# Gated rows transposed in 32x32 squares on VectorE, with transfers between partitions, and two steps of the z stage in another order

## The chip, the cores and the metric

The kernel runs on one core of one Trainium2 chip. A core has five engines that run their own instruction queues and wait for one another through semaphores: TensorE (PE; its weight loads are shown apart as PEld), VectorE (DVE), ScalarE (ACT), GpSimd (POOL) and SyncE (SP), which here issues nearly all transfers between DRAM and the on-chip memory SBUF. Products of TensorE land in PSUM, eight banks per partition. The metric is device time in microseconds; lower is better.

## The reference

A block of a transformer, all in float32: attention with 32 heads on a normalised x, added to x, then a gated MLP (gMLP) on the normalised sum. The change lies in the second half:

```python
h = x + _A_ref(_layernorm(x, axis=-1), A_wqkv, A_wo)
h2 = h + _B_ref(_layernorm(h, axis=-1), B_w_in, B_w_sp, B_b_sp, B_w_out)

def _B_ref(x, w_in, w_sp, b_sp, w_out):      # S = 2048 rows, D = 512, Fh = 688
    z = _gelu(jnp.einsum("bsd,df->bsf", x, w_in))
    z1 = z[..., :Fh]
    z2 = _layernorm(z[..., Fh:], axis=-1)
    g = jnp.einsum("ts,bsf->btf", w_sp, z2) + b_sp[None, :, None]
    return jnp.einsum("bsf,fd->bsd", z1 * g, w_out)
```

## The kernel before

Three stages follow one another. The first, attention, is not touched. Rows of x are handled in 16 blocks of 128 (`NB`); block p and block p+8 form pair p. Numbers in float32 are multiplied as sums of two float16 parts, a high and a low one, with three products each (`mm3`, lines 106 to 109; its lines 107, 108 and 109 are the three matmuls).

**The second stage** (loop over k at line 1242) takes the row blocks in the order 0, 1, 8, 9, 2, 10, 3, 11 and so on to 7, 15. For step k it makes h for the block two steps ahead (`make_h`), makes z for its own block in four pieces of 344 columns (`make_z(sb, 1, 0)`, `(1, 1)`, `(0, 0)`, `(0, 1)`: the first index is 1 for the half that is normalised, 0 for the half z1), and transposes the next block's normalised h on TensorE (`turn`, line 1175), which ScalarE and VectorE split into the parts hT (lines 98 and 104). Normalising needs 1/sqrt of a variance, a chain of some ten small VectorE instructions (`rstd_of`, lines 114 to 126, then nb at line 766) before ScalarE applies it; for h that gives hn (line 1268). `gate_z` (line 1203) does the same for z: z1 is stored to DRAM (z_scr, issued by ScalarE), the chain runs on VectorE, ScalarE normalises z2 (line 1212), and GpSimd mostly forms sums, differences and float16 parts of it, tiles b11, t1, t2, b22, t3, b21, n4, which are the operands of the spatial product in Strassen-like form (two levels of 2x2 blocks, seven products). One of those subtractions, for b21 of the lower block of a pair, is kept in the list `subs` and run on VectorE in the next step.

**The last stage** (loop over p) runs over the eight pairs. For a pair TensorE makes seven products of 24 matmuls (`product`), named after their operands: b11, t1, t2, b22, t3, b21, n4, into three PSUM banks A, C, B, the later ones adding to what stands there. Each consumes one 512 KB operand from a ring (`op`, nine buffers), and at its end asks for the operand eight products ahead. ScalarE and VectorE empty the banks, GpSimd multiplies with z1; the two gated rows of the pair stand in `pr` (row index w = 0, 1). Columns 0 to 383 are half 0, the rest half 1. For each half: `level` finds the largest magnitude per row (a reduction and three small instructions on VectorE), `raise_` scales the rows by a power of two on ScalarE, `turn` transposes three 128x128 blocks per row on TensorE into PSUM (line 1379; for half 1 GpSimd first copies 64 columns, so that the last block is whole), `split` makes the float16 parts pT from PSUM (high part on ScalarE, line 1387, low part on VectorE, lines 1388 and 1391), `multiply` multiplies them with w_out into a PSUM bank (acc, two buffers), and `gather` adds the result to h on VectorE (line 1408), which `store` writes out.

The order of the instructions on each engine, in both stages, is the order in which the code is written (`manual_schedule`); no scheduler moves them. A pair's `turn(1)` stands at its own end, behind n4, and its `multiply(1)`, `turn(0)` and `multiply(0)` stand in the next pair, behind products b11 and t1. Every transfer waits, besides its data, for the transfer issued eight places before it, since eight semaphores are used in turn.

Of the kernel before, what the change touches and what calls it, by code (L numbers as in the profile page):

```python
# [8 lines left out]
F32 = mybir.dt.float32  # L9
F32R = mybir.dt.float32r  # L10
BF = mybir.dt.bfloat16
F16 = mybir.dt.float16
# [47 lines left out]
def block_kernel(ctx: ExitStack, tc: tile.TileContext, x, wqkv, wo, w_in, w_sp4, b_sp, w_out, out):  # L60
# [1103 lines left out]
    with ExitStack() as mid:  # L1164
# [33 lines left out]
            else:  # L1198
                sub(nc.gpsimd if el == "pool" else nc.vector)

        subs = []

        def gate_z(sb, meanwhile):

# [33 lines left out]
        with tc.manual_schedule(engines={E.PE, E.Activation, E.DVE, E.Pool, E.SP}):  # L1238
# [3 lines left out]
            for k in range(NB):  # L1242
                sb, new = row[k], row.get(k + 2)
                if new is not None:
                    for _ in make_h(new, ps.tile([P, 512], F32, name="acc")):
                        pass
                if k + 3 < NB:
                    split_o(row[k + 3])
                new_z(sb)
                make_z(sb, 1, 0)  # L1250
                if k + 1 < NB and k != NB - 2:
                    turn(row[k + 1])
                if subs:
                    subs.pop()(nc.vector)
                if new is not None:
                    mv, rs = scale_h(new)
                    nb = minus_mean(e2, mv, rs)
                make_z(sb, 1, 1)
                if k == NB - 2:
                    turn(row[k + 1])  # L1260
                for c in range(2):
                    nc.vector.bn_stats(zst[sb][:, c, :], zs[sb][1][:, c * FC:(c + 1) * FC])
                make_z(sb, 0, 0)
                make_z(sb, 0, 1)
                hTs.pop(sb)
                if new is not None:
                    hns[new] = e2.tile([P, D], F32, name="hn", bufs=3)
                    nc.scalar.activation(hns[new], xrs.pop(new), AF.Identity, bias=nb, scale=rs)
                if k == 1:
                    invert()  # L1270
                if k >= NB - 8:
                    ask()

                def meanwhile():
                    if k + 4 < NB:
                        asked.pop(0)()
                    if k + 5 < NB:
                        asked.append(load_o(row[k + 5]))

                gate_z(sb, meanwhile)  # L1280
    early.close()
    late.close()

# [1 line left out]
    with ExitStack() as fin:  # L1285
# [52 lines left out]
        class Rows:  # L1338
# [26 lines left out]
            def lower(self, half, *which):  # L1365

                for w in which:
                    d = self.downs[half, w]
                    nc.vector.tensor_scalar(d, d, 2.0 ** -14, w_down, op0=ALU.mult, op1=ALU.mult)

            def turn(self, half, w):

                if half:
# [7 lines left out]
            def split(self, half, w):  # L1381

                tp, n = self.turned.pop((half, w)), 3 - half
                if half not in self.pT:
                    self.pT[half] = [f2.tile([P, 2, 3, P], F16, name=f"pT{half}{i}") for i in range(2)]
                hi, lo = self.pT[half]
                nc.scalar.activation(hi[:, w], tp[:, :3], AF.Copy)
                nc.vector.tensor_sub(lo[:, w, :n], tp[:, :n], hi[:, w, :n])
# [36 lines left out]
        with tc.manual_schedule(engines={E.PE, E.Activation, E.DVE, E.Pool, E.SP}):  # L1425
# [9 lines left out]
            for p in range(HB):  # L1435
# [8 lines left out]

                product(A, "b11")
                nc.scalar.activation(p1, A, AF.Identity, bias=bt)
                if p:
                    accs = [before.multiply(1, w) for w in range(2)]
                    for w in range(2):
                        before.turn(0, w)  # L1450
                        before.gather(1, w, accs[w])
                        before.split(0, w)
                    before.lower(0, 0, 1)
                product(C, "t1")
                nc.scalar.activation(q5, C, AF.Identity, bias=bb)
                if p:
                    accs = [before.multiply(0, w) for w in range(2)]
                    for w in range(2):
                        before.gather(0, w, accs[w])
                        before.store(w)  # L1460
                else:
                    weigh_w()
                product(A, "t2", False)
                nc.scalar.activation(v, A, AF.Identity, bias=bt)
                product(C, "b22", False)
                nc.vector.tensor_add(right, C, v)  # L1466
                nc.gpsimd.tensor_mul(right, right, z1t[:, FC:])  # L1467
                if not p:
                    measure_w()
                product(A, "t3", False)  # L1470
                nc.vector.tensor_add(br, A, q5)
                (nc.vector if last else nc.gpsimd).tensor_mul(br, br, z1b[:, FC:])
                now.level(1, 0, 1)
                now.raise_(1, 0, 1)
                product(B, "b21")
                nc.vector.tensor_add(left, B, p1)
                (nc.vector if last else nc.gpsimd).tensor_mul(left, left, z1t[:, :FC])
                if last:
                    now.level(0, 0)
                    for w in range(2):  # L1480
# [1 line left out]
                        now.split(1, w)  # L1482
                    now.lower(1, 0, 1)
                    now.raise_(0, 0)
                product(A, "n4", False)
                nc.vector.scalar_tensor_tensor(bl, A, bb, z1b[:, :FC], op0=ALU.add, op1=ALU.mult)
                if last:
                    now.level(0, 1)
                    now.raise_(0, 1)
                else:  # L1490
                    now.level(0, 0, 1)
                    for w in range(2):
                        now.turn(1, w)
                        now.split(1, w)
                    now.lower(1, 0, 1)
                    now.raise_(0, 0, 1)
            accs = [now.multiply(1, 0)]
            now.turn(0, 0)
            now.split(0, 0)
# [42 lines left out]
```

## Time and profile before

| what | us |
|---|---|
| median of 3 runs (lowest, highest) | 1726.86 (1726.46, 1728.48) |
| the profiled execution | 1726.86 |
| its span, first to last instruction | 1725.1 |
| busy: TensorE / VectorE / ScalarE / GpSimd | 1708.8 / 1438.4 / 1318.7 / 815.5 |
| attention, up to the first block of h turned (about) | 0 to 1295 |
| second stage: first turn (1294.60) to the start of b11 (1455.22) | 161 |
| last stage: to the end of the span | 270 |
| one pair of the last stage (turn to turn, 1513.28 to 1546.4) | 33.15 |
| granted TensorE clock | 1.000 |

A row of a timeline has the start, the duration, the engine, the line of the kernel, the operation, the tiles written and read, the shape and a count of like instructions drawn together; in brackets stands how long the engine was idle before it, and on whom it waited. A row that groups instructions has, behind the bar, busy us in total, the mean in ns and the idle time in front of them; where three numbers stand with slashes, they are the least, the median and the largest duration in ns, then the first and last start. A row of waits has the engine and tile that waited, the one waited for, the sum in us, the number of times and the longest. SPq and ACTq are the queues in which transfers are issued; a duration there is that of the issue.

### The profile page before, as it was taken

Reading aid. Unit: us, or ns where it says so; the run is one execution under the profiler, and the core shown is the slowest. Engines: PE = TensorE matmul, PEld = TensorE weight load, DVE = VectorE, ACT = ScalarE, POOL = GpSimd, SP = SyncE. Lnnn points to the kernel's source line nnn. Section 1 sums busy time; section 2 is a strip of 40 time slices with the busy share of each in tenths; the row PEclk is TensorE's granted clock in tenths of the full one; section 3 lists DMA queues with packets and bytes.
Section 4 is the critical chain, followed back from the end, with each engine's and each line's share of the span. In section 5 each row is a group of like instructions: output and inputs, shape, how many; then the busy total and the mean of one; then the engine's idle time right before and its main releaser. Section 6 shows DMA issues by size and latency. Waiting matters only on the chain.

```text
span 1725.1 us, 36747 instructions
## 1 busy us (share of the span) xinstructions
PE 1708.8 (99%) x13583; PEld 653.4 (38%) x13583; DVE 1438.4 (83%) x3030; ACT 1318.7 (76%) x2598; POOL 815.5 (47%) x1076
## 2 busy tenths in 40 slices
PE   9999999999999999999999999999999999999999
PEld 4433222222222222222222222222216566666665
DVE  7688999999999999999999999999927886433234
ACT  4334999999999999999999999999994554221111
POOL 1231867776672267687677866400013766110010
PEclk9999999999999999999999999999999999999999
DMA  5534332342231234344345343300124464654540
GB/s 183 162 97 144 101 88 69 100 98 81 75 71 27 60 105 117 113 149 135 103 121 146 115 147 103 80 20 12 45 51 135 136 184 159 228 179 145 170 139 25
DMA packets 183932, 190.51 MB, mean 110 GB/s; under 512 B 65704, under 2 KB 134632, under 8 KB 183752
## 3 DMA queue, kind: packets, MB, share of 16 engines
q1 hardware_dynamic: 181448, 182.53, 36.2%
q10 hardware_dynamic: 2304, 5.64, 0.8%
q8 instruction: 106, 1.74, 0.4%
q14 instruction: 74, 0.61, 0.1%
HBM read 122.10 MB, written 65.93 MB: 109 GB/s over the span
## 4 chain that ended last, share of the span: by engine, by line
PE 76%; DVE 15%; DMA 3%; ACT 2%; issue 2%; POOL 2%; SPq 1%; DVEq 0%; ACTq 0%; POOLq 0%
PE pv L828 26%; PE s L803 17%; PE m L223 9%; DVE mx L228 7%; PE acc L107 4%; PE g L109 4%; PE g L108 4%; PE g L107 4%; PE acc L109 3%; PE acc L108 3%; DVE ab L237 1%; DMA rc<-r_scr 1%; DVE og L838 1%; DVE rs_t L124 1%; DVE rs_u L126 1%
## 5 line engine op out<-in xcount | busy, mean ns | idle before, releaser
L812 ACT ACTIVATE pt<-s 128x512 f32<-128x512 f32 x1968 | 1006.3, 637 | 5.1 <-PE m L223 4.0
L228 DVE TENSOR_REDUCE mx<-m 128x1 f32<-128x512 f32 x1510 | 947.5, 682 | 12.6 <-PE m L223 3.9
L803 PE MATMUL s<-qst,kst 50*128 50x512 f16 x2048 | 604.3, 379 | 0.2
L828 PE MATMUL pv<-pt,vst 128*32 128x256 f32 (+1 forms) x6056 | 598.1, 466 | 4.1 <-DVE og L838 1.3
L223 PE MATMUL m<-kst,qst 48*128 48x512 f16 x1510 | 452.4, 381 | 0.0
L803 PEld LDWEIGHTS <-kst 50*128 50x128 f16 x2048 | 131.9, 94 | 352.1 <-issue 323.7
L828 PEld LDWEIGHTS pv<-pt,vst 128*32 128x32 f32 x6056 | 119.5, 108 | 290.3 <-issue 276.9
L223 PEld LDWEIGHTS <-qst 48*128 48x128 f16 x2048 | 159.2, 93 | 173.7 <-issue 124.3
L223 PE MATMUL m<-uvs,qst 48*128 48x512 f16 x504 | 190.5, 380 | 0.3 <-DVE mx L228 0.3
L245 POOL TENSOR_SCALAR nm<-nm 128x16 f32<-128x16 f32 x32 | 6.6, 206 | 359.7 <-DVE nm L242 359.7
L237 DVE CUSTOM_DVE_ANT_0 ab<-m,ab 128x512 f32<-128x512 f32 x252 | 170.5, 677 | 2.7 <-ACT ab L233 2.7
L233 ACT ACTIVATE ab<-m 128x512 f32<-128x512 f32 x252 | 157.3, 624 | 16.5 <-PE m L223 15.8
L989 POOL TENSOR_TENSOR op<-raw,op 128x512 f16<-128x512 f32 x80 | 92.9, 1161 | 6.0
L1467 POOL TENSOR_TENSOR pr<-pr,z 128x344 f32<-128x344 f32 x8 | 7.3, 912 | 176.9 <-DVE pr L1466 173.0
L912 POOL TENSOR_TENSOR raw<-raw 128x512 f32<-128x512 f32 (+1 forms) x84 | 83.3, 991 | 6.7
L917 POOL TENSOR_TENSOR acc_sp<-acc_sp,raw 128x512 f32<-128x512 f32 x63 | 80.5, 1277 | 4.5
L107 PE MATMUL acc<-wi,hT 128*128 128x344 f16 x256 | 79.1, 309 | 1.4 <-ACT hT L98 1.4
L1362 ACT ACTIVATE pr<-pr,up 128x304 f32<-128x304 f32 (+1 forms) x32 | 17.0, 574 | 81.9 <-DVE up L1316 81.9
L109 PE MATMUL acc<-wi,hT 128*128 128x344 f16 x256 | 79.1, 309 | 0.3 <-DVE hT L104 0.3
L108 PE MATMUL acc<-wi,hT 128*128 128x344 f16 x256 | 79.1, 309 | 0.0
L1408 DVE SCALAR_TENSOR_TENSOR h<-acc,low,h 128x512 f32<-128x512 f32 (+1 forms) x33 | 24.1, 732 | 45.8 <-PE acc L109 32.5
L909 POOL TENSOR_SCALAR raw<-raw 128x512 f32<-128x512 f32 (+1 forms) x88 | 52.3, 594 | 19.5 <-DMA raw<-in_wqkv 12.2
(240 smaller groups left out, 2280.1 us busy)
## 6 DMA issues: line engine op xcount, KB each, us to landing
raw<-in_w_sp SPq DMA_DIRECT2D x128, 256.0 KB
s_scr<-op SPq DMA_DIRECT2D x64, 256.0 KB
op<-s_scr SPq DMA_DIRECT2D x32, 512.0 KB
a_scr<-op SPq DMA_DIRECT2D x48, 256.0 KB
op<-a_scr SPq DMA_DIRECT2D x24, 512.0 KB
o_scr<-og SPq DMA_DIRECT2D x64, 128.0 KB
qst<-q_scr SPq DMA_DIRECT2D x192, 32.0 KB
kst<-k_scr SPq DMA_DIRECT2D x48, 128.0 KB
```

What stands on the lines that cost most here:

```text
L107: nc.tensor.matmul(ps, lh, rh, start=first, stop=False, **kw)
L108: nc.tensor.matmul(ps, lh, rl, start=False, stop=False, **kw)
L109: nc.tensor.matmul(ps, ll, rh, start=False, stop=last, **kw)
L223: nc.tensor.matmul(acc, q[r, p, c], keys[r, p], start=True, stop=True)
L228: nc.vector.reduce_max(at(t, e if t else e - 1), acc, axis=AX.X)
L233: nc.scalar.activation(ab[0], acc, AF.Abs)
L237: nc.vector.tensor_tensor_reduce(ab[0], acc, ab[0], 0.5, LOW, ALU.add, ALU.max, at(0, 0))
L803: nc.tensor.matmul(s, kst[hg % 2][r, p, kb * P:(kb + 1) * P], qst[hg * NQ + qb][r, p, :], start=True, stop=True)
L812: nc.scalar.activation(pts[p, kb][:, t, :], s, AF.Exp, scale=scales_[hg // 2])
L828: nc.tensor.matmul(pv[0][32 * j:32 * j + 32, a:b], vst[hg % 2][:, c:c + 32], pts[j % 2, kb][:, j // 2, a:b], start=kb == 0, stop=kb == NB - 1,
L912: pool.tensor_mul(got[0] if n else acc, got[0], got[0])
L989: chores.append((lambda: pool.tensor_sub(t[0][:, 1], of(), t[0][:, 0]), TT))
```

## The change

In the last stage, pairs 0 to 6 no longer transpose on TensorE. `squares` transposes the 32x32 squares of the scaled rows on VectorE, within groups of 32 partitions, into one tile for the pair; `send` issues 16 transfers of 48 KB from SBUF to SBUF that bring each square to the partitions where it belongs (`whole`); `hi` and `lo` make the float16 parts from there, on ScalarE and VectorE. The rows are still multiplied with w_out during the next pair, but behind product b21 rather than behind b11 and t1, and stored behind n4. Pair 7 still transposes on TensorE. The tiles pT have one buffer each instead of two.

In the second stage the late subtraction of b21 (`subs`) runs behind the 1/sqrt chain of h rather than ahead of it, and the gate work of the third last block (k = 13, block 14) runs in step k = 14, behind the turn of the last block, instead of at the end of its own step.

```diff
@@ -1198,7 +1198,7 @@
             else:
                 sub(nc.gpsimd if el == "pool" else nc.vector)
 
-        subs = []
+        subs, put_off = [], []
 
         def gate_z(sb, meanwhile):
 
@@ -1250,14 +1250,15 @@
                 make_z(sb, 1, 0)
                 if k + 1 < NB and k != NB - 2:
                     turn(row[k + 1])
-                if subs:
-                    subs.pop()(nc.vector)
                 if new is not None:
                     mv, rs = scale_h(new)
                     nb = minus_mean(e2, mv, rs)
+                if subs:
+                    subs.pop()(nc.vector)
                 make_z(sb, 1, 1)
                 if k == NB - 2:
                     turn(row[k + 1])
+                    put_off.pop()()
                 for c in range(2):
                     nc.vector.bn_stats(zst[sb][:, c, :], zs[sb][1][:, c * FC:(c + 1) * FC])
                 make_z(sb, 0, 0)
@@ -1271,13 +1272,16 @@
                 if k >= NB - 8:
                     ask()
 
-                def meanwhile():
+                def meanwhile(k=k):
                     if k + 4 < NB:
                         asked.pop(0)()
                     if k + 5 < NB:
                         asked.append(load_o(row[k + 5]))
 
-                gate_z(sb, meanwhile)
+                if k == NB - 3:
+                    put_off.append(lambda sb=sb, then=meanwhile: gate_z(sb, then))
+                else:
+                    gate_z(sb, meanwhile)
     early.close()
     late.close()
 
@@ -1368,6 +1372,49 @@
                     d = self.downs[half, w]
                     nc.vector.tensor_scalar(d, d, 2.0 ** -14, w_down, op0=ALU.mult, op1=ALU.mult)
 
+            def squares(self, half):
+
+                if half:
+                    self.sq = f2.tile([P, 4, 2, 2, 3, 32], F32, name="squares", bufs=1)
+                t = self.sq[:, :, half]
+                if half:
+                    for w in range(2):
+                        nc.vector.transpose(t[:, :, w, :2].rearrange("p q i a -> p i q a"),
+                                            self.pr[:, w, HF:HF + 2 * P])
+                    for q in (0, 2):
+                        nc.vector.transpose(t[:, q:q + 2, :, 2].rearrange("p q w a -> p w q a"),
+                                            self.pr[:, :, FH - TW:FH])
+                else:
+                    nc.vector.transpose(t.rearrange("p q w i a -> p (w i) q a"), self.pr[:, :, :HF])
+
+            def send(self):
+
+                self.whole = f2.tile([P, 4, 2, 2, 3, 32], F32, name="whole", bufs=1)
+                for j in range(4):
+                    for q in range(4):
+                        nc.sync.dma_start(self.whole[32 * q:32 * q + 32, j], self.sq[32 * j:32 * j + 32, q])
+
+            def hi(self, half):
+
+                src = self.whole[:, :, half].rearrange("p j w i a -> p (w i) j a")
+                self.pT[half] = [f2.tile([P, 2, 3, P], F16, name=f"pT{half}{i}", bufs=1) for i in range(2)]
+                nc.scalar.activation(self.pT[half][0].rearrange("p w i (j a) -> p (w i) j a", a=32), src, AF.Copy)
+
+            def lo(self, half):
+
+                src, (hi, lo) = self.whole[:, :, half], [
+                    t.rearrange("p w i (j a) -> p w i j a", a=32) for t in self.pT[half]]
+                if not half:
+                    lo, src, hi = [t.rearrange(f"p {d} -> p (w i) j a")
+                                   for t, d in ((lo, "w i j a"), (src, "j w i a"), (hi, "w i j a"))]
+                    nc.vector.tensor_sub(lo, src, hi)
+                    return
+                src = src.rearrange("p j w i a -> p w i j a")
+                for w in range(2):
+                    nc.vector.tensor_sub(lo[:, w, :2], src[:, w, :2], hi[:, w, :2])
+                t = hi[TW:, :, 2]
+                nc.vector.tensor_sub(t, src[TW:, :, 2], t)
+
             def turn(self, half, w):
 
                 if half:
@@ -1382,7 +1429,7 @@
 
                 tp, n = self.turned.pop((half, w)), 3 - half
                 if half not in self.pT:
-                    self.pT[half] = [f2.tile([P, 2, 3, P], F16, name=f"pT{half}{i}") for i in range(2)]
+                    self.pT[half] = [f2.tile([P, 2, 3, P], F16, name=f"pT{half}{i}", bufs=1) for i in range(2)]
                 hi, lo = self.pT[half]
                 nc.scalar.activation(hi[:, w], tp[:, :3], AF.Copy)
                 nc.vector.tensor_sub(lo[:, w, :n], tp[:, :n], hi[:, w, :n])
@@ -1444,37 +1491,40 @@
 
                 product(A, "b11")
                 nc.scalar.activation(p1, A, AF.Identity, bias=bt)
-                if p:
-                    accs = [before.multiply(1, w) for w in range(2)]
-                    for w in range(2):
-                        before.turn(0, w)
-                        before.gather(1, w, accs[w])
-                        before.split(0, w)
-                    before.lower(0, 0, 1)
                 product(C, "t1")
                 nc.scalar.activation(q5, C, AF.Identity, bias=bb)
-                if p:
-                    accs = [before.multiply(0, w) for w in range(2)]
-                    for w in range(2):
-                        before.gather(0, w, accs[w])
-                        before.store(w)
-                else:
+                if not p:
                     weigh_w()
                 product(A, "t2", False)
                 nc.scalar.activation(v, A, AF.Identity, bias=bt)
+                if p:
+                    before.lower(1, 0, 1)
+                    before.lower(0, 0, 1)
                 product(C, "b22", False)
                 nc.vector.tensor_add(right, C, v)
                 nc.gpsimd.tensor_mul(right, right, z1t[:, FC:])
-                if not p:
+                if p:
+                    before.hi(1)
+                    before.hi(0)
+                else:
                     measure_w()
                 product(A, "t3", False)
                 nc.vector.tensor_add(br, A, q5)
                 (nc.vector if last else nc.gpsimd).tensor_mul(br, br, z1b[:, FC:])
+                if p:
+                    before.lo(1)
+                    before.lo(0)
                 now.level(1, 0, 1)
                 now.raise_(1, 0, 1)
+                if not last:
+                    now.squares(1)
                 product(B, "b21")
                 nc.vector.tensor_add(left, B, p1)
                 (nc.vector if last else nc.gpsimd).tensor_mul(left, left, z1t[:, :FC])
+                if p:
+                    accs = [before.multiply(1, w) for w in range(2)]
+                    for w in range(2):
+                        before.gather(1, w, accs[w])
                 if last:
                     now.level(0, 0)
                     for w in range(2):
@@ -1482,18 +1532,23 @@
                         now.split(1, w)
                     now.lower(1, 0, 1)
                     now.raise_(0, 0)
+                if p:
+                    accs = [before.multiply(0, w) for w in range(2)]
+                    for w in range(2):
+                        before.gather(0, w, accs[w])
                 product(A, "n4", False)
                 nc.vector.scalar_tensor_tensor(bl, A, bb, z1b[:, :FC], op0=ALU.add, op1=ALU.mult)
+                if p:
+                    for w in range(2):
+                        before.store(w)
                 if last:
                     now.level(0, 1)
                     now.raise_(0, 1)
                 else:
                     now.level(0, 0, 1)
-                    for w in range(2):
-                        now.turn(1, w)
-                        now.split(1, w)
-                    now.lower(1, 0, 1)
                     now.raise_(0, 0, 1)
+                    now.squares(0)
+                    now.send()
             accs = [now.multiply(1, 0)]
             now.turn(0, 0)
             now.split(0, 0)
```

Three places show how the instructions now stand.

VectorE in one pair of the last stage, before, from the eviction br of product t3 (pr<-g,q) over the level of half 1, the eviction left (pr<-g,p) and the eviction bl, to the level of half 0:

```order
L1471 TENSOR_TENSOR pr<-g,q_23672 128x344
L1351 TENSOR_REDUCE low_23870<-pr 128x2
L1313 TENSOR_SCALAR low_23870<-low_23870 128x2
L1314 TENSOR_SCALAR low_23870<-low_23870 128x2
L1316 TENSOR_SCALAR up_23871<-low_23870 128x2
L1476 TENSOR_TENSOR pr<-g,p_23670 128x344
L1486 SCALAR_TENSOR_TENSOR pr<-g,fig_1843,z_23357 128x344
L1351 TENSOR_REDUCE low_23933<-pr 128x2
```

Now, from the same eviction br to the first gather (h<-acc):

```order
L1512 TENSOR_TENSOR pr<-g,q_23676 128x344
L1414 TENSOR_TENSOR pT_23791<-whole,pT_23790 128x256 x2
L1416 TENSOR_TENSOR pT_23790<-whole,pT_23790 64x2x128
L1410 TENSOR_TENSOR pT_23794<-whole,pT_23793 128x768
L1355 TENSOR_REDUCE low_23828<-pr 128x2
L1317 TENSOR_SCALAR low_23828<-low_23828 128x2
L1318 TENSOR_SCALAR low_23828<-low_23828 128x2
L1320 TENSOR_SCALAR up_23829<-low_23828 128x2
L1382 STREAM_TRANSPOSE squares<-pr 128x2x4x32 x2
L1385 STREAM_TRANSPOSE squares<-pr 128x2x2x32 x2
L1522 TENSOR_TENSOR pr<-g,p_23674 128x344
L1455 SCALAR_TENSOR_TENSOR h_23090<-acc,low_23524,h_23090 128x512
```

Behind br now stand the four low parts of the pair before, read from whole, and behind the level the four transposes; left and the first gather come after them.

SP's queue over one pair, before (z and h are loads for the next pair, op the operands, out_y the stores):

```order
L1421 DMA z_23355<-z_scr 128x688
L1421 DMA z_23357<-z_scr 128x688
L1421 DMA h_23359<-h_scr 128x512
L1421 DMA h_23361<-h_scr 128x512
L1161 DMA op<-s_2_scr 128x2048 x2
L1411 DMA out_y<-h_23082 128x512
L1411 DMA out_y<-h_23084 128x512
L1161 DMA op<-s_2_scr 128x2048 x2
L1161 DMA op<-a_2_scr 128x2048 x2
L1161 DMA op<-a_3_scr 128x2048
```

Now:

```order
L1395 DMA whole<-squares 32x384 x16
L1468 DMA z_23358<-z_scr 128x688
L1468 DMA z_23360<-z_scr 128x688
L1468 DMA h_23362<-h_scr 128x512
L1468 DMA h_23364<-h_scr 128x512
L1161 DMA op<-s_2_scr 128x2048 x4
L1161 DMA op<-a_2_scr 128x2048 x2
L1161 DMA op<-a_3_scr 128x2048
L1458 DMA out_y<-h_23082 128x512
L1458 DMA out_y<-h_23084 128x512
```

The 16 transfers of the pair before stand ahead of the loads, and the stores have moved behind the pair's last operand.

ScalarE in step k = 14 of the second stage, before (hn of the last block; then the gate of step 13: store, normalising, two casts; then z and hT of the last block):

```order
L1268 ACTIVATE hn<-xr,nb,rs_u 128x512
L1207 DMA z_scr<-z_22714 128x688
L1212 ACTIVATE z_22715<-z_22715,nb,rs_u 128x688
L1194 CAST b_0_20668<-z_22715 128x344
L1194 CAST b_0_20666<-z_22715 128x344
L1190 ACTIVATE z_22840<-acc,fig_1841 128x344 x2
L98 ACTIVATE hT_22876<-tp 128x512
```

Now:

```order
L1269 ACTIVATE hn<-xr,nb,rs_u 128x512
L1190 ACTIVATE z_22807<-acc,fig_1841 128x344 x2
L98 ACTIVATE hT_22842<-tp 128x512
L1207 DMA z_scr<-z_22714 128x688
L1212 ACTIVATE z_22715<-z_22715,nb,rs_u 128x688
L1194 CAST b_0_20668<-z_22715 128x344
L1194 CAST b_0_20666<-z_22715 128x344
```

The gate's four instructions have moved behind hT of the last block.

## The prediction

> **What bounds the kernel now.** Read first, the waits of TensorE over the second stage and the stretches of the last one (columns: PE, its weight loads, VectorE, ScalarE, GpSimd busy us, then granted clock, DMA share, GB/s):
>
> ```profile
> span 1725.1 us, 36747 instructions
> PE tp L1175 <- ACT hn L1268: 1.6, 5, 0.7
> PE acc L107 <- ACT hT L98: 1.4, 1, 1.4
> PE acc L109 <- DVE hT L104: 0.3, 1, 0.3
> ...
> 1500.00:1550.00 50.00, 50.00 (x334) 32.69 (x332) 16.66 (x41) 8.41 (x18) 6.18 (x10) 1.00 0.52 169
> 1650.00:1700.00 50.00, 50.00 (x317) 31.11 (x315) 15.01 (x35) 8.01 (x16) 3.09 (x5) 1.00 0.25 88
> ```
>
> The last stage is TensorE from end to end: it never waits there, at clock 1.00, while VectorE is busy a third of the time. So an instruction taken off TensorE is worth its full length, and a wait given to TensorE costs its full length. In the second stage TensorE does wait, a little. The timeline of TensorE at one pair's end gives the prices:
>
> ```profile
> 1509.78 0.31 PE L107 MATMUL g<-n,op 128*128 128x344 f16 x1
> ...
> 1513.28 0.82 PE L1379 MATMUL tp<-ident,pr 128*128 128x128 f32 x6
> 1513.93 0.31 PE L107 MATMUL g<-b,op 128*128 128x344 f16 x1
> ...
> 1517.43 0.38 PE L107 MATMUL acc<-wu,pT 128*128 128x512 f16 x1
> ...
> 1520.88 0.82 PE L1379 MATMUL tp<-ident,pr 128*128 128x128 f32 x6
> ```
>
> By starts, since ends are modelled: a product of 24 matmuls takes 1513.28-1509.78 = 3.50 us, six transposes 0.65, the 16 matmuls of multiply(1) for both rows 3.45 (0.216 each). The 18 of multiply(0) then take 3.89.
>
> **Removed: the transposes.** Pairs 0 to 6 lose 12 each, fourteen groups of six: 14 x 0.65 = 9.1 us off TensorE. The GpSimd copies that go with them ran beside it and are worth nothing.
>
> **Added: a line of work on VectorE, between t3 and the second multiply.** After product t3 VectorE now runs br, four subtractions (lo), level(1), the transposes in squares(1), left, and only then gather(1,0). With two banks for acc, multiply(0,0) cannot start before gather(1,0) has emptied the first. So I time that line, with T the start of b11, from this piece of the timelines:
>
> ```profile
> 1506.28 0.31 PE L107 MATMUL g<-b,op 128*128 128x344 f16 x1
> 1506.48 0.52 DVE L1471 TENSOR_TENSOR pr<-g,q 128x344 f32<-128x344 f32 x1 [2.91 <-PE g L109]
> 1507.07 0.91 POOL L1472 TENSOR_TENSOR pr<-pr,z 128x344 f32<-128x344 f32 x1 [2.51 <-DVE pr L1471]
> 1508.02 0.79 DVE L1351 TENSOR_REDUCE low<-pr 128x2 f32<-128x608 f32 x1 [1.02 <-POOL pr L1472]
> 1509.25 0.17 DVE L1316 TENSOR_SCALAR up<-low 128x2 int32<-128x2 int32 x1
> 1509.51 0.99 ACT L1362 ACTIVATE pr<-pr,up 128x304 f32<-128x304 f32 x2 [9.49 <-DVE up L1316]
> ...
> L1388 DVE TENSOR_TENSOR pT<-tp,pT 128x256 f16<-128x256 f32 x16 | 6.7, 421 | 0.2
> L1351 DVE TENSOR_REDUCE low<-pr 128x2 f32<-128x768 f32 x7 | 6.7, 953 | 0.7
> L1351 DVE TENSOR_REDUCE low<-pr 128x2 f32<-128x608 f32 x8 | 6.3, 786 | 7.5 <-POOL pr L1472 7.4
> L1408 DVE SCALAR_TENSOR_TENSOR h<-acc,low,h 128x512 f32<-128x512 f32 x31 | 23.2, 748 | 44.6 <-PE acc L109 31.3 <-PE acc L1403 13.1
> L1195 DVE TENSOR_TENSOR b<-z,b x7: 516/1094/1096, 1335.7 to 1446.4; 128x344 f16<-128x344 f32 x7
> ```
>
> t3 ends at T+17.5 (five products); br starts 0.2 later (1506.48 against 1506.28) and ends at T+18.2. The four lo, three of 256 elements per partition at 0.42 and one of 768 at 0.95, make 2.2: T+20.4. But lo now reads two tiles in SBUF, where before one was in PSUM, and GpSimd's product for br (0.91, from 0.59 after br's start) falls on it. The last row is the nearest: the same kind of subtraction took 516 ns alone and 1094 in its median case, with GpSimd at work. I add one GpSimd product, 0.85: T+21.25. The reduction and its three small instructions take 1.40 (1508.02 to 1509.42): T+22.65; ScalarE's two scalings start 0.1 later and end at T+23.75. squares(1) has four transposes of 256, 256, 128 and 128 elements per partition; the first hides behind the second scaling.
>
> Their price is not in the trace for this type. Lower bound: the two reductions differ by 160 elements and 0.167 us, so 0.00104 per element on a base of 0.15, giving 0.42 and 0.28. Upper bound: twice the part that grows, 0.69 and 0.42. The nearest row is a transpose of half the width, which stands by the base and shows no fill time, so I take the lower:
>
> ```profile
> L259 DVE STREAM_TRANSPOSE mturned<-mparts x32: 199/201/211, 143.9 to 1252.2; 128x32 f16<-128x32 f16 x32
> ```
>
> The Trainium skill (Vector Engine (DVE) Microarchitecture Reference, section 3.8) says that the transposing front end sustains one element per cycle per lane; by that the sum is mine, and no run here shows it for four bytes yet.
>
> Three more transposes, 0.98, bring T+24.7; left 0.5: T+25.2; gather(1,0) 0.75: T+25.95. TensorE ended b21 at T+21.0 and multiply(1) at T+24.45. It waits till about T+25.9 (instructions overlap by up to 0.1): **1.4 us per pair**. After that gathers fit between multiplies (1.94 each), and left, bl and the pair's other evictions have slack. Without the collision the wait is 0.55; with the dear transposes 2.2.
>
> This holds for pairs 1 to 6. Pair 0 has nothing to multiply. In pair 7 there is no squares(1) and GpSimd is idle beside lo: br and its product end at T+18.8, lo at T+21.0, level(1) at T+22.3, left and its product T+23.3, gather(1,0) T+24.1, before T+24.45. So 6 x 1.4 = 8.4 us are given back.
>
> The Trainium skill (SBUF — State Buffer, Who interferes with whom) speaks against this change: a VectorE instruction with two SBUF inputs and a GpSimd instruction that reads SBUF exclude each other, and the later one waits for the whole of the other. The 1094 ns agree. By the rule the wait is 1.4 a pair, without it 0.55, and the sum 5 us lower.
>
> **Added: 16 transfers per pair, and what they pass.** squares(0) waits for n4's end, bl, level(0) and the scaling:
>
> ```profile
> 1513.48 0.57 DVE L1486 SCALAR_TENSOR_TENSOR pr<-g,fig,z 128x344 f32<-128x344 f32 x1 [2.98 <-PE g L109]
> 1515.82 1.12 ACT L1362 ACTIVATE pr<-pr,up 128x384 f32<-128x384 f32 x2 [1.14 <-DVE up L1316]
> ...
> 1514.45 0.90 SPq L1421 DMA_DIRECT2D h<-h_scr  x2
> ...
> 1252.40 0.33 SPq L260 DMA_DIRECT2D m_scr<-mturned  x1
> 1254.66 1.34 SPq L263 DMA_DIRECT2D qst<-m_scr  x2
> ```
>
> Scaling ends 3.7 after n4 (1516.94-1513.28); the 768-element transpose adds 0.95 (as the reduction): T+4.7 of the next pair. Sixteen issues at 0.33 to 0.45 make 6.4, and a small transfer that another waits for is there 2.3 after its issue (1252.40 to 1254.66): all landed near T+13.3. Each also waits for the transfer eight places ahead; at 2.3 us that one is done. hi(1) and hi(0) follow on ScalarE, about 1.05 each, done at T+15.4, well ahead of T+18.2. Behind the 16 in SP's queue stand the z and h loads and four operand loads, now some 10 us later; operands are asked eight products (28 us) ahead and z, h are for the next pair, so that costs nothing; were operands late, it would show as TensorE waiting on op.
>
> **Moved: the second stage.** The late subtraction of b21 stood ahead of the 1/sqrt chain; now it stands behind it:
>
> ```profile
> 1428.65 1.09 DVE L1195 TENSOR_TENSOR b<-z,b 128x344 f16<-128x344 f32 x1
> 1431.92 0.21 DVE L766 TENSOR_SCALAR nb<-rs_u,mv 128x1 f32<-128x1 f32 x1
> 1432.17 0.81 ACT L1268 ACTIVATE hn<-xr,nb,rs_u 128x512 f32<-128x512 f32 x1 [2.85 <-DVE nb L766]
> ...
> 1432.50 0.31 PE L109 MATMUL acc<-wi,hT 128*128 128x344 f16 x1
> 1433.03 0.44 PE L1175 MATMUL tp<-ident,hn 128*128 128x128 f32 x2 [0.23 <-ACT hn L1268]
> ```
>
> hn comes 1.0 us earlier, more than the longest of the five waits (0.7). A shown wait is short by 0.16, since matmuls start every 0.146 but are drawn 0.31 long: 1.6 + 5 x 0.16 = 2.4 us. The subtraction itself has a pair's time to spare.
>
> The gate of row 13 is put behind the turn of row 15. ScalarE did it ahead of hT(15):
>
> ```profile
> 1441.12 0.33 ACTq L1207 DMA_DIRECT2D z_scr<-z  x1
> 1444.50 0.96 ACT L1212 ACTIVATE z<-z,nb,rs_u 128x688 f32<-128x688 f32 x1 [2.58 <-DVE nb L766]
> 1447.13 0.59 ACT L98 ACTIVATE hT<-tp 128x512 f16<-128x512 f32 x1
> 1447.78 0.32 PE L107 MATMUL acc<-wi,hT 128*128 128x344 f16 x1 [1.40 <-ACT hT L98]
> 1453.54 0.84 POOL L1195 TENSOR_TENSOR b<-z,b 128x344 f16<-128x344 f32 x1
> ```
>
> hT(15) can start once its transposes are done, near 1442.9, so both hT waits go: 1.40 + 0.26 + 2 x 0.16 = 2.0. What is late next: the gate's 1/sqrt starts after hT's lo, 2.3 us later, and with it GpSimd's parts. The gate's store of z moves too, from 1441.12 to about 1443.6; the one z tile that it reads is rewritten near 1448.5, so it stays covered. Row 13's b21 subtraction moves to the next row's turn, long before the last stage's b21. b11's last low part, 1453.54 to 1454.38 here, then comes near 1456.6, while TensorE, 2 us ahead, wants it near 1456.4: 0.2 is given back. Gain 4.2; bounds 0 (if GpSimd is later than that) and 4.4.
>
> **Sum.** 1725.1 - 9.1 + 8.4 - 4.2 = 1720.2 us of span. The profiled execution took 1726.86, 1.8 over its span and equal to the median: **1722.0 us**. About 0.2% (3.5 us) is what a measurement can tell from no change, so this is just faster.
>
> **Rivals.** *VectorE's line is cheaper* (18%): no collision, so 0.55 per pair: 1722.0 - 5.1 = 1717; hidden wholly, 1713.6. For it: GpSimd could be held back instead. Against: level(1) needs that very product.
>
> *Dear squares* (20%): transposes at twice the part per element, or VectorE keeping GpSimd out through all four lo, so that level(1) starts 1 us later: 2.2 to 2.4 a pair, 1727 to 1728. For it: nothing in the trace prices either.
>
> *The transfers land late* (14%, the slower side). It decides from T+17: each us beyond delays hi, lo and all behind it by 1 us, six times. If each took 7 us, as the 1280 KB load of raw_w does, the second eight wait for the first: T+4.7+7+2.8+7 = T+21.5, lo starts at T+22.6, 4.4 late less the 0.85 collision: 6 x 3.6 = 21 more, 1743. Against: DMA share is half.
>
> ```profile
> 1455.52 0.38 SPq L1430 DMA_DIRECT2D raw_w<-in_w_out  x1
> 1463.57 3.65 DVE L1322 TENSOR_REDUCE w<-raw_w 128x1 f32<-128x512 f32 x6 [3.29 <-DMA raw_w<-in_w_out]
> ```
>
> *The moved gate gains nothing* (6%): GpSimd's parts hold b11 as long as the waits were: 1726.
>
> **Chances.** My case has 42%, and its own range 1719 to 1725 from a wait of 1.0 to 1.9; six parts in seven of it lie under 1723.4. Faster: 36 + 18 = 54%. Within 0.2%: 6 + 20 + 6 = 32%. Slower: 14%. The range from 1715 to 1730 holds all but late transfers and a wholly hidden line.
>
> **What would show it.** L1379's count falls from 96 to 12. TensorE's waits in the last stage: one of about 1.4 us per pair on gather (h), six times, ahead of multiply(0,0); none on op, pT or p. The lo subtractions of 256 elements: one of the three near 1.3 us, or GpSimd's product near 1.3 or longer. Transposes of 256 elements 0.42 us against 0.69. In the second stage the waits on hn and hT are gone. Wrong if TensorE waits for hi (late transfers), or if gather(1,0) ends before multiply(1) does.

## The result, and the profile after

The changed kernel takes **1720.37 us** (median of 6 runs, 1719.88 to 1720.95) where the kernel before took 1727.07 beside it (6 runs, 1725.97 to 1728.48): ratio 0.9963, 95% interval 0.9953 to 0.9973. The forecast was 1722.0 us, with 1719 to 1725 as its own case's range; the gain is 6.7 us where 4.9 was forecast.

The waits of TensorE in the changed kernel, whose span is now 1718.6 us, first over the second stage (1285 to 1452 us), then, behind the dots, over the last one (from 1452 us); columns: what waited for what, us in total, times, longest:

```profile
PE acc L109 <- DVE hT L104: 0.3, 1, 0.3
PE acc L745 <- DVE og L838: 0.2, 1, 0.2
...
PE acc L107 <- DVE h L1455: 5.0, 6, 1.0
```

The five waits on hn and the wait of 1.4 us on hT(15) are gone. A wait on hT of 0.3 is still there, but it is another: it stands ahead of z of row 14, at 1437.90 us. In the last stage there are six waits, all on h (the gather), none on pT, op or p. Each is 0.16 longer than shown, since matmuls start every 0.216 us and are drawn 0.38: 5.0 + 6 x 0.16 = 6.0 us, 1.0 a pair.

Two stretches of the last stage of the changed kernel (PE, its weight loads, VectorE, ScalarE, GpSimd busy us, clock, DMA share, GB/s):

```profile
1500.00:1550.00 50.00, 48.23 (x302) 29.38 (x301) 20.91 (x48) 7.68 (x15) 3.76 (x4) 1.00 0.54 199
1650.00:1700.00 50.00, 49.23 (x314) 30.63 (x312) 20.62 (x46) 9.31 (x16) 4.36 (x6) 1.00 0.38 126
```

TensorE, busy throughout before, now has holes: 1.8 us in the first stretch, which holds two of the waits, and 0.8 in the second, which holds one. The groups of the instructions that the change touches (busy us, mean ns | idle before, and who ended it), over the last stage:

```profile
L1426 PE MATMUL tp<-ident,pr 128*128 128x128 f32 x12 | 1.8, 272 | 0.0
L1382 DVE STREAM_TRANSPOSE squares<-pr 128x256 f32<-128x256 f32 x14 | 6.2, 446 | 4.8 <-ACT pr L1366 4.8
L1385 DVE STREAM_TRANSPOSE squares<-pr 128x128 f32<-128x128 f32 x14 | 3.2, 270 | 0.0
L1388 DVE STREAM_TRANSPOSE squares<-pr 128x768 f32<-128x768 f32 x7 | 6.8, 978 | 8.7 <-ACT pr L1366 8.7
L1414 DVE TENSOR_TENSOR pT<-whole,pT 128x256 f16<-128x256 f32 x14 | 9.2, 702 | 0.6 <-ACT pT L1401 0.5
L1513 POOL TENSOR_TENSOR pr<-pr,z 128x344 f32<-128x344 f32 x7 | 7.1, 1021 | 14.9 <-DVE pr L1512 14.8
```

Of 96 transposes on TensorE 12 are left, those of pair 7. VectorE's transposes cost the lower bound of the prediction. The lo subtractions of 256 elements take 702 ns in the mean where 421 was the price of the like subtraction before, and GpSimd's product 1021 where it took 912: the two run into each other, as the experiment on lo below shows.

One pair's line in the changed kernel, from the timelines of VectorE, SyncE's queue, ScalarE and TensorE; T, the start of b11, is 1510.02 here:

```profile
1510.02 0.31 PE L107 MATMUL g<-b,op 128*128 128x344 f16 x1
...
1513.71 0.98 DVE L1388 STREAM_TRANSPOSE squares<-pr 128x768 f32<-128x768 f32 x1 [1.25 <-ACT pr L1366]
...
1514.72 10.71 SPq L1395 DMA_DIRECT2D whole<-squares  x16
1526.81 1.57 ACT L1401 ACTIVATE pT<-whole 128x768 f16<-128x768 f32 x2 [5.49 <-DMA whole<-squares]
...
1527.72 0.52 DVE L1512 TENSOR_TENSOR pr<-g,q 128x344 f32<-128x344 f32 x1 [2.91 <-PE g L109]
1528.15 1.46 DVE L1414 TENSOR_TENSOR pT<-whole,pT 128x256 f16<-128x256 f32 x2
1529.63 0.42 DVE L1416 TENSOR_TENSOR pT<-whole,pT 64x256 f16<-64x256 f32 x1
1530.08 0.96 DVE L1410 TENSOR_TENSOR pT<-whole,pT 128x768 f16<-128x768 f32 x1
1530.96 0.78 DVE L1355 TENSOR_REDUCE low<-pr 128x2 f32<-128x608 f32 x1
...
1533.02 0.88 DVE L1382 STREAM_TRANSPOSE squares<-pr 128x256 f32<-128x256 f32 x2 [0.67 <-ACT pr L1366]
1533.83 0.46 DVE L1385 STREAM_TRANSPOSE squares<-pr 128x128 f32<-128x128 f32 x2
1534.21 0.48 DVE L1522 TENSOR_TENSOR pr<-g,p 128x344 f32<-128x344 f32 x1
1534.62 1.39 DVE L1455 SCALAR_TENSOR_TENSOR h<-acc,low,h 128x512 f32<-128x512 f32 x2
...
1535.40 0.38 PE L107 MATMUL acc<-wu,pT 128*128 128x512 f16 x1 [0.76 <-DVE h L1455]
```

It is the line of the prediction, instruction for instruction, between br and the gather; the last row is multiply(0,0), which waits for that gather. What differs: the sixteen issues take 10.7 us, not 6.4, so hi starts at T+16.8 where T+13.3 was forecast, and both hi are done at T+18.4, just behind the end of br at T+18.2. This is one pair of seven. Over the seven, hi starts between T+16.3 and T+17.8 (mean T+17.0), and in the first of them VectorE's lo waits for it:

```profile
1494.72 0.52 DVE L1512 TENSOR_TENSOR pr<-g,q 128x344 f32<-128x344 f32 x1 [2.92 <-PE g L109]
1495.71 1.14 DVE L1414 TENSOR_TENSOR pT<-whole,pT 128x256 f16<-128x256 f32 x2 [0.48 <-ACT pT L1401]
```

For the experiments two lengths are read from each timeline of TensorE: the second stage, from its first transpose of hn to b11's first matmul, and the last stage, from there to the span's end. Before: 160.6 and 269.9. After: 157.2 and 266.5. So each half of the change gives about 3.4 us. In this kernel and the seven below that keep both moves the second stage lies between 156.7 and 157.9 us: two executions can differ by about 1 us in this length, and smaller differences are read from the waits instead.

### The profile page after: what moved, and what is told of

Read it like the earlier page. It is cut to its first block, busy times and chain, and to the rows that moved or that the text cites. A ratio compares the mean times of both kernels' runs of the same rounds, so it can differ in the third digit from the quotient of the medians.

```text
span 1718.6 us, 36670 instructions
## 1 busy us (share of the span) xinstructions
PE 1699.9 (99%) x13499; PEld 643.9 (37%) x13499; DVE 1452.8 (85%) x3051; ACT 1317.3 (77%) x2584; POOL 813.8 (47%) x1062
## 4 chain that ended last, share of the span: by engine, by line
PE 65%; DVE 16%; DMA 5%; issue 5%; SPq 4%; POOL 3%; ACT 2%; DVEq 0%; ACTq 0%; POOLq 0%
PE pv L828 26%; PE s L803 17%; PE m L223 9%; DVE mx L228 7%; PE acc L107 3%; PE acc L109 3%; PE acc L108 3%; SPq L1395 2%; DMA rc<-r_scr 2%; DVE ab L237 1%; DMA z_scr<-z 1%; DVE og L838 1%; PE g L108 1%; PE g L109 1%; PE g L107 1%
## 5 line engine op out<-in xcount | busy, mean ns | idle before, releaser
L894 POOL TENSOR_SCALAR raw<-raw,figs 128x512 f32<-128x512 f32 (+1 forms) x84 | 55.8, 668 | 8.8 <-DMA raw<-in_wo 7.9
```

## The experiments

**Each half of the change by itself.** The first kernel is the kernel before with the change's edits to the second stage; the second is the changed kernel with the same edits undone:

```diff
-                if subs:
-                    subs.pop()(nc.vector)
                 if new is not None:
                     mv, rs = scale_h(new)
                     nb = minus_mean(e2, mv, rs)
+                if subs:
+                    subs.pop()(nc.vector)
...
                     turn(row[k + 1])
+                    put_off.pop()()
...
-                gate_z(sb, meanwhile)
+                if k == NB - 3:
+                    put_off.append(lambda sb=sb, then=meanwhile: gate_z(sb, then))
+                else:
+                    gate_z(sb, meanwhile)
```

> The kernel before with the second stage's two moves alone (b21's late subtraction behind the 1/sqrt chain, row 13's gate behind the turn of row 15); the last stage as before. Theory: the moves take 3.5 to 4.2 us by themselves, because TensorE's five waits on hn and the one on hT(15) go and only one short wait on hT comes: 1722.8 to 1723.6 us, with the start of the last stage's first product some 3.5 us earlier. Rival: a part of it is lost again at the last stage's start, where b11 waits for GpSimd's late low part, and the squares hid that: 1724.5 us or more.

> The changed kernel with the second stage in its old order: only the squares and their transfers. Theory: 9.1 us of transposes go from TensorE and six waits of 1.0 us on gather come back, so 3.1 us less than before: about 1723.8 us, and six waits on h of about 1 us in the last stage. Rival (the prediction's price of 1.4 a wait holds when the last stage starts later): about 1726.2 us.

The second stage alone: 1724.12 us, ratio 0.9986 (0.9977 to 0.9995), stage lengths 157.4 and 270.1. The squares alone: 1723.04 us, ratio 0.9979 (0.9970 to 0.9988), lengths 160.2 and 266.4, six waits on h of 5.3 us shown. The halves add up and neither hides the other: the first changes only the first length (the last one is 270.1 against 269.9), the second only the last one. By its median the first came 0.5 us above its range and the second 0.8 below its figure, both inside what the intervals allow.

**The two moves of the second stage apart.** The kernel before with the lines on subs of this diff alone, and with those on put_off alone. Each has a single run, 1725.60 and 1725.11 us, beside 1726.56 for the kernel before (10 runs).

> The kernel before with b21's late subtraction behind the 1/sqrt chain, and nothing else. Theory: the five waits on hn (1.6 us shown, 2.4 real) go, the wait of 1.4 us on hT(15) stays; second stage 2.2 to 2.6 us shorter than the kernel before's. Rival: z's 1/sqrt chain, now behind the subtraction, makes ScalarE's gate late and with it hT of later rows: new waits on hT of 1 us or more in the second stage, and less than 1.2 us gained.

> The kernel before with row 13's gate behind the turn of row 15, and nothing else. Theory: the wait of 1.4 us on hT(15) and the 0.3 behind it go, the five waits on hn stay, and about 0.25 us comes back at b11 or not at all, since TensorE is 2.4 us later than in the changed kernel and GpSimd's low part is then in time: second stage 1.6 to 2.0 us shorter. Rival: the short wait on hT(14), seen in the changed kernel, comes with this move: it is here too, and the gain is 1.3 us or less.

The waits of TensorE over the second stage, with the subtraction moved alone, and then with the gate moved alone:

```profile
PE acc L107 <- ACT hT L98: 1.6, 1, 1.6
PE acc L109 <- DVE hT L104: 0.5, 2, 0.3
PE acc L745 <- DVE og L838: 0.2, 1, 0.2
```

```profile
PE tp L1175 <- ACT hn L1269: 1.6, 5, 0.7
PE acc L745 <- DVE og L838: 0.2, 1, 0.2
```

The subtraction alone shortens the stage by 1.6 us (159.0), less than the 2.2 to 2.6 expected; the gate alone by 2.1 (158.5), a little more than expected. Both misses are smaller than the 1 us by which two executions differ, so the waits decide. The new short wait on hT(14) comes with the subtraction (two waits on hT L104 there, none with the gate), so the rival of the second run falls. That of the first is right in kind but not in size: z's 1/sqrt chain now runs behind the subtraction, ScalarE does z's normalisation, some 1 us later than before, ahead of hT(14), and hT(14) is late; that costs 0.4 (0.26 shown and 0.16), and the wait on hT(15) is 0.2 longer (1.64 against 1.40).

**The gathers ahead of squares(1).** In the changed kernel, in the last stage's loop:

```diff
                 now.raise_(1, 0, 1)
-                if not last:
-                    now.squares(1)
                 product(B, "b21")
...
                     for w in range(2):
                         before.gather(1, w, accs[w])
+                if not last:
+                    now.squares(1)
```

> The changed kernel with squares(1) put behind the two gathers of half 1, where VectorE did them ahead of the gathers. Theory: the six waits of about 1.0 us are squares(1) standing ahead of gather(1,0) and nothing else; with them behind it TensorE does not wait in the last stage at all: 6 us less than the changed kernel, about 1714.4 us, and squares(1) is hidden beside multiply(0). Rival: lo and its collision with GpSimd hold the gather too, or the wait moves to gather(0,0) or to a later product: a wait of 0.5 us or more per pair stays, 1717 to 1720 us.

1714.22 us, ratio 0.9928 (0.9915 to 0.9942), and no wait of TensorE in the last stage. The same stretch, and VectorE in the same pair (T is 1510.15):

```profile
1500.00:1550.00 50.00, 50.00 (x313) 30.46 (x312) 21.45 (x52) 8.53 (x15) 3.77 (x4) 1.00 0.55 203
```

```profile
1532.39 0.51 DVE L1520 TENSOR_TENSOR pr<-g,p 128x344 f32<-128x344 f32 x1
1533.08 0.75 DVE L1455 SCALAR_TENSOR_TENSOR h<-acc,low,h 128x512 f32<-128x512 f32 x1 [0.18 <-PE acc L1450]
1534.80 0.75 DVE L1455 SCALAR_TENSOR_TENSOR h<-acc,low,h 128x512 f32<-128x512 f32 x1 [0.98 <-PE acc L1450]
1535.47 0.76 DVE L1382 STREAM_TRANSPOSE squares<-pr 128x256 f32<-128x256 f32 x2
1536.16 0.46 DVE L1385 STREAM_TRANSPOSE squares<-pr 128x128 f32<-128x128 f32 x2
```

The wait has changed sides: the gather now waits for TensorE (0.18 and 0.98), and squares(1) runs beside multiply(0). The last stage takes 260.5 us, 6.0 less than in the changed kernel: exactly the six waits. It is also 9.4 less than before, and since no wait is left, that is the price of the 84 transposes (9.1 in the prediction). The collision is still there (683 ns for lo in the mean) and costs nothing.

**The collision on lo.** GpSimd's product for br is put on VectorE in every pair:

```diff
-                (nc.vector if last else nc.gpsimd).tensor_mul(br, br, z1b[:, FC:])
+                nc.vector.tensor_mul(br, br, z1b[:, FC:])
```

> The changed kernel with br's product with z (0.5 us of VectorE) on VectorE instead of GpSimd in every pair. Theory: one of each pair's lo subtractions takes 1.0 us instead of 0.42 because it collides with that product on GpSimd; without it all three take 0.42, the added product fits mostly into the time in which VectorE waits for hi, and TensorE's wait falls by 0.2 to 0.4 us: 1718 to 1719.3 us. Rival: the 1.0 us has another cause (the first lo is slow after the transfers, or waits for hi in part): it stays, the wait grows by 0.3 to 0.5 us, and the time is 1722 to 1723.4 us.

1719.27 us, ratio 0.9956 (0.9943 to 0.9970), an interval that overlaps the changed kernel's; the last stage is 265.1 us against 266.5. The group of lo subtractions of this kernel in the last stage, and TensorE's waits there:

```profile
L1414 DVE TENSOR_TENSOR pT<-whole,pT 128x256 f16<-128x256 f32 x14 | 5.3, 418 | 0.0
```

```profile
PE acc L107 <- DVE h L1455: 3.7, 6, 0.6
```

Without GpSimd beside them all lo take 418 ns, so it was the product that made one of each pair long: 9.2 - 5.3 = 3.9 us of busy time over six pairs, 0.65 each. The product, now on VectorE, puts the start of lo off by 0.55 (T+18.7 against T+18.1 in the same pair), and the wait falls by 0.2 a pair. The Trainium skill (SBUF — State Buffer, Who interferes with whom) states this as a lock between a VectorE instruction with two SBUF inputs and a GpSimd one that reads SBUF; the 418 against 702 ns agree.

**Later transfers.** Four more transfers of 48 KB per pair, into a tile that nothing reads, issued ahead of the sixteen; then, in another kernel, the sixteen put behind the next loads of z and h in the queue:

```diff
+                self.spare = f2.tile([P, 4, 2, 2, 3, 32], F32, name="spare", bufs=1)
+                for q in range(4):
+                    nc.sync.dma_start(self.spare[32 * q:32 * q + 32, 0], self.sq[:32, q])
                 for j in range(4):
```

```diff
                 before, now = now, Rows(p, (ht, hb))
+                if p:
+                    before.send()
...
                     now.squares(0)
-                    now.send()
```

> The changed kernel with four more transfers of 48 KB per pair, into a tile that nothing reads, issued ahead of the sixteen. Theory: SP issues them one after the other at 0.6 us, the sixteen land 2.5 us later (T+19.3), there is almost no slack, and lo starts 2.0 us later, less the 0.6 of the collision with GpSimd, which is past by then: TensorE waits 1.4 us more per pair, in part on hi or lo (pT) ahead of multiply(1), about 2.4 us per pair in all, six or seven times: 1729 to 1732 us. Rival: the landing has 2 us or more of slack, or the issues overlap: 1720.4 to 1722 us and the same six waits.

> The changed kernel with the sixteen transfers issued behind the next pair's loads of z and h in SP's queue, where they stood ahead of them. Theory: the four loads are issued while SP waits for squares(0) anyway, so the sixteen are issued from the same time and land at T+16 to T+17.5; the burst of delayed loads after them gets smaller: 1719.7 to 1721.5 us, the same six waits of 1.0 us. Rival: the loads in front hold the lanes or the DMA engines, the sixteen land 2 us or more later and each us costs six: 1728 us or more.

With four more: 1733.81 us (1731.17 to 1735.37), ratio 1.0037 (1.0023 to 1.0052), slower than before. Its waits in the last stage, and then three stretches that each begin as a wait ends:

```profile
PE acc L107 <- DVE h L1458: 15.2, 6, 2.9
PE tp L1429 <- ACT pr L1366: 0.5, 1, 0.5
```

```profile
1503.80:1507.40 3.60, 3.60 (x10) 1.28 (x10) 0.58 (x1) 0.00 (x0) 0.26 (x1) 0.53 1.02 413
1540.00:1543.60 3.60, 3.60 (x17) 1.62 (x17) 1.31 (x2) 0.00 (x0) 0.24 (x1) 1.00 1.03 419
1575.00:1578.60 3.60, 3.60 (x11) 1.35 (x11) 0.88 (x2) 0.00 (x0) 0.19 (x1) 0.59 1.03 418
```

The six waits grow from 6.0 to 15.2 + 6 x 0.16 = 16.2 us, 1.7 a pair. All of it falls on the gather; none falls on pT, where I had expected a part. The rest, 4.6 us of the 14.8 by which the last stage is longer (281.3), is pair 7 (about 1) and, unforeseen, the clock: after the two longest waits, 2.87 us shown, the granted clock is 0.53 and 0.59, and 16 matmuls start every 0.43 us instead of 0.216, 3.3 us in all. After the next longest, 2.71, it stays at 1.00:

```profile
1574.91 0.38 PE L107 MATMUL acc<-wu,pT 128*128 128x512 f16 x1 [2.87 <-DVE h L1458]
1645.80 0.38 PE L107 MATMUL acc<-wu,pT 128*128 128x512 f16 x1 [2.71 <-DVE h L1458]
```

That accounts for most of what lies above the expected range: without it this execution, 1734.45 us, would be near 1731. Over the five runs the time goes with the mean clock: 1734.45 and 1735.37 us at 0.998, 1731.17 to 1733.81 at 0.999.

With the loads in front: 1720.99 us (1720.21 to 1721.39), ratio 0.9968 (0.9956 to 0.9981), the same six waits (5.1 us shown); the sixteen are issued from 1514.57 and hi starts at 1526.89, T+17.0, as in the changed kernel. SyncE has the time for the loads while it waits for squares(0).

**Both edits as a version to keep, and how much slack the gathers leave.**

> The gathers ahead of squares(1) and the loads of z and h ahead of the sixteen transfers, both at once, as a version to keep. Theory: TensorE already waits for nothing in the last stage once the gathers come first, so the second edit adds nothing: 1714.2 us again (1713.5 to 1715), no wait on h. Rival: the two interact (the transfers land later beside the loads while the gathers no longer cover it): 1716 us or more.

> The gathers ahead of squares(1), with the four more transfers of 48 KB per pair ahead of the sixteen. Theory: the landing sets the line in front of the gather: lo at T+20.6 as in the run with four more transfers, level(1) done at T+24.1, left and gather(1,0) at T+25.3, 0.85 behind multiply(1)'s end, so a wait of 0.8 to 0.9 us per pair on h and 1 us more in the last pair: 1719.5 to 1721 us; the slack that the gathers first leave to the transfers is 1.6 us, no more. Rival: with the gathers first the landing no longer matters: 1714.2 to 1715.5 us, no wait.

The gathers first and the loads first: 1714.55 us (1714.22 to 1714.79), ratio 0.9930 (0.9916 to 0.9943), nothing over the gathers first alone. With the four more transfers: 1719.08 us, ratio 0.9955 (0.9940 to 0.9970), last stage 5.0 us longer. Its waits in the last stage:

```profile
PE acc L107 <- ACT pr L1366: 2.9, 5, 0.9
PE tp L1429 <- ACT pr L1366: 0.5, 1, 0.5
```

The name is to be read with care. At 1633.28 us multiply(0,0) goes on; ScalarE's scaling ends 0.04 earlier and is named, but what the matmul needs is its bank, and the gather that empties it ends in the same tenth. A wait of 0.74 a pair on five pairs (2.9 + 5 x 0.16 = 3.7) was a little less than expected. The four transfers that added 10.2 us of such waits to the changed kernel add 3.7 here. Pair by pair the wait follows the landing: none where hi starts at T+18.9, 0.20 shown at T+19.3, 0.94 at T+20.2. So it begins near T+19, while hi starts at T+17.0 in the mean with the gathers first alone: an estimate of 2 us of slack from these rows, a little more than the 1.6 expected.

## Why the prediction was right, point by point

**The transposes removed:** right, 9.1 against 9.4 measured by the run with the gathers first.

**The line on VectorE:** the mechanism, its place and its number (six) were right; the term was too large, 1.4 a pair against 1.0, 8.4 against 6.0 in all. In the pair shown lo ended at T+21.0 (forecast 21.25), level(1) at T+22.3 (22.65), squares(1) at T+24.3 (24.7), left at T+24.7 (25.2), and the gather at T+25.35 (25.95). The collision was 0.65 and not the 0.85 of a whole GpSimd product, and the rest is that consecutive VectorE instructions overlap: the next one starts up to 0.1 us before the end of the one ahead (1534.62 against 1534.69 above), which I had named and taken off once in the sum, not at each step. The measured 1.0 lies half way between the 1.4 forecast and the 0.55 of the rival of a cheaper line, whose condition, no collision, did not hold; the rival of dear transposes is wrong: 446, 270 and 978 ns against 0.42, 0.28 and 0.95 us.

**The transfers:** the step "sixteen issues at 0.33 to 0.45 make 6.4" failed: they took 10.7, and hi started at T+17.0 in the mean, not T+13.3, right at the T+17 given as the point from which it decides. (Each hi took 0.83 us, not 1.05, so in the trace that point is nearer T+17.3.) TensorE never waited for hi or pT, as forecast, but in the two latest pairs (T+17.8 and T+17.4) lo started late, and their waits on the gather are 1.00 and 0.95 shown where the other four are 0.76 to 0.79. That this term cost almost nothing was luck: 3.7 us of margin were forecast and none were there. The price was in view: the rows quoted in the prediction hold, beside the transfer of 0.33, two of 0.67 each (qst<-m_scr, 1.34 for both), and 16 x 0.67 is 10.7. The four more transfers bear out the slope: hi starts 2.8 us later in the mean and each pair waits 1.7 longer, the 0.65 of the collision being saved. So the rival of late transfers was much nearer than its argument (a DMA share of half) let it seem. (Its price for a slow transfer, 7 us, is low too: the load of raw_w quoted there begins to be issued at 1455.52 and is waited for until 1463.57, 8.05 us.)

**The second stage:** 3.4 us of 4.2 came in the changed kernel; the mean of the eight that keep both moves (157.4) lies 3.0 under that of the two that keep neither (160.6 before, 160.2 with the squares alone). The five waits on hn and the wait on hT(15) went, and b11 waits for GpSimd's low part as forecast (that part ends at 1455.54, and TensorE's next matmul starts at 1455.59, behind a gap of 0.09 in the records, about 0.25 with the drawing of matmuls taken off). What failed is the phrase that the subtraction "has a pair's time to spare": the subtraction has, but the z chain behind it has not, and hT(14) pays 0.4. Small waits of 0.1 on hn, below what the view of waits lists, are left on three rows.

**The sum:** with the measured terms, -9.4 + 6.0 - 3.4 = -6.8, against -6.7 by the medians and -4.9 forecast. The number owes something to luck too: the wait was 2.4 us too dear and the second stage 0.8 too generous, and the two errors partly cancel.

## What to carry to other kernels

Where work is moved from the engine that bounds to one with time to spare, what counts is the order on the second engine: here the line of VectorE ahead of the instruction that frees TensorE's bank was paid for as far as it outlasted multiply(1), 1.0 us a pair, and one statement put behind that instruction nearly doubled the gain (1720.4 to 1714.2 us). Price a row of small transfers by the queue's issue time for that very kind of transfer, and find how far its landing is from the point where it decides before calling it hidden.

## What the hardware did that I had not expected

- A transfer of 48 KB from SBUF to SBUF took SyncE 0.59 us to issue in the median, one behind another every 0.63, and in the pair shown one of the sixteen took 1.28: 10.71 / 16 = 0.67 in the mean (0.60 for the four spare ones, 2.42 us in all). That is twice the 0.33 of the store m_scr<-mturned in the trace of before and as much as its load qst<-m_scr. What sets the price of an issue no run here shows.
- TensorE's granted clock halved after a wait of 2.87 us shown (3.0 with the 0.16), both times, and did not after the four waits of 2.71 or less. The matmul of 512 columns then started every 0.43 us for about 3.4 us. The Trainium skill (TensorE: Matmul & The Clock Gate, Part 1) gives 426.7 and 215.7 ns for the two clocks, which agrees; it speaks of an idle window of about 3.4 us, and here a wait about 0.4 us shorter was enough.
